# Attention with a learned distance bias and two feed-forward stages on one core: two query buffers, late clearing of probability tiles, smaller rings in the bias stretch

## The chip, the cores and the metric

The kernel runs on one core of one Trainium2 chip. The metric is the device time of one execution in microseconds (us). The core has TensorE (PE; PEld is its weight load), VectorE (DVE), ScalarE (ACT), GpSimd (POOL) and SyncE (SP), each with its own instruction queue worked off in order, and 16 DMA engines that share what is issued. In this kernel SyncE issues every transfer.

## What is computed

Attention over 2 batches, 8 heads, 576 positions, head size 64, with a bias that a small network makes from the distance of two positions, and then two feed-forward stages on the 1152 rows of 512. All is float32.

```python
scores = scale * np.matmul(q, k.transpose(0, 1, 3, 2))
psi_rel = np.log1p(np.abs(rel))                       # rel = i - j
psi_i = np.log1p(np.maximum(pos[:, None], 1.0))
x = (psi_rel / psi_i)[..., None]
h = np.maximum(x @ w1 + b1, 0.0)                      # 32 hidden units
bias = h @ w2                                         # one value per head
scores = scores + bias.transpose(2, 0, 1)[None, :, :, :]
attn = softmax(scores)
x = attn @ v                                          # rows of 8 heads x 64 = 512
x = (silu(x @ w_gate) * (x @ w_val)) @ w_out          # 512 -> 1536 -> 512
out = softplus(x @ w_in) @ w_out2                     # 512 -> 2048 -> 512
```

## The kernel before

**Precision.** Matmuls run on pairs of reduced-precision tiles: a high part and a remainder (`kst` holds both halves of the keys, `qh` and `ql` the queries' two parts). `high` is a cast on ScalarE or VectorE, `low` a subtraction, mostly on GpSimd.

**The bias stretch.** 36 blocks, in the order 32 to 35 and then 0 to 31. For each block `hidden` writes four tiles `r` (three on VectorE, the fourth on ScalarE) from a table `G`; `second` multiplies them with the second layer's weights, eight matmuls into a PSUM tile `pb` of two; `keep` scales `pb` on ScalarE into a tile `st` and has SyncE send it off. `r` comes from a pool `rp` of 12 buffers, `st` from `stp` of 4; a buffer is written again when its last reader is done, for `st` when its transfer has landed. `hidden` runs two blocks ahead, and its `r` on ScalarE stands ahead of the `st` of the block two back. The first four blocks go to a tensor `last` in device memory and come back, other way round, by two `bias<-last` transfers that wait for all four; the other 32 go straight to the tiles `bias` (0 to 3), eight to each.

**Attention.** Eight units, each one pair of heads of one batch. A unit has keys `kr` (two transfers of 288 KB), queries `qr` (two of 288 KB), values `v` (256 KB) and `vt` (32 KB). It has two halves (`sub` 0 and 1) of four and five slots. A slot does the scores of one 128-row chunk into `ps`, adds the bias and takes the row minimum on VectorE (`biased`, writes a tile `e` of 128x640 of which 576 columns are used), exponentials on ScalarE, and the normalization on GpSimd (`softmax`). Later slots transpose `e` (`transposes`, `gather`) and multiply by the values (`values`). The transposes read the 64 columns behind the 576th too, so these hold zeros. There are 14 tiles `e`, five of them from the start, nine after the bias stretch, in the room of `G`, `r` and `st`; each tile's last columns are cleared on GpSimd when the tile is made (line 128).

**What runs where.** The first five slots of unit 0 are run inside the bias stretch, behind the blocks numbered 23, 26, 31, 33 and 35 (`EARLY`). `prep` is a generator with the casts and subtractions of the next half's `kst`, `qh` and `ql`; two of its steps go into each slot. The order on TensorE, ScalarE, VectorE and GpSimd is that of the program text; SyncE's order is a scheduler's.

**Loads.** `kr` and `qr` have one buffer each (pool `qkraw`). `load_k` of the next unit is called at the first slot of a unit, `load_qv` (queries and values) at the first slot of its second half.

After attention come the weight stages: 68 weight tiles are loaded, turned into two parts and multiplied on TensorE. The change does not touch them.

Of the kernel before, what the change touches and what calls it, by code (L numbers as in the profile page):

```python
# [11 lines left out]
F32 = mybir.dt.float32  # L12
# [7 lines left out]
P = 128  # L20
B, H, S, D, HID = 2, 8, 576, 64, 32
# [64 lines left out]
def tile_kernel(ctx: ExitStack, tc, qT, kT, vS, wb, wg, wv, wo, wi, wo2, table, out):  # L86
    nc = tc.nc
# [13 lines left out]
    def opener(stack):  # L101
        return lambda name, bufs, **k: stack.enter_context(
            tc.tile_pool(name=name, bufs=bufs, reuse_waits="tile", **k)
        )

    with ExitStack() as actx:
        pool = opener(actx)
        biasp = pool("biasp", 1)
        bias = [biasp.tile([P, H, S], F32, name=f"bias{c}") for c in range(4)]
        bias.append(biasp.tile([P, NP, S], F32, name="bias4"))  # L110
        rawp = pool("qkraw", 1)
        kp = pool("kp", 2)
        qp = pool("qp", 1)
        vp = pool("vp", 2)
# [6 lines left out]
        es = []  # L121

        def new_es(name, count):

            ep = pool(name, 1)
            for _ in range(count):
                es.append(ep.tile([P, 5 * P], F32, name=f"e{len(es)}"))
                nc.gpsimd.memset(es[-1][:, S:], 0.0)

        new_es("ep0", 5)  # L130
        psS = pool("psS", 2, space=PSUM)

        def load(r, src, pr, b):
            for d in range(2):
                sp.dma_start(
                    out=r[D * d : D * (d + 1)], in_=src[b, 2 * pr : 2 * pr + 2].rearrange("h d s -> d h s")
                )

        def load_k(pr, b):
            kr = rawp.tile([P, 2, S], F32, tag="kr", name="kr")  # L140
            load(kr, kT, pr, b)
            return dict(pr=pr, b=b, kr=kr)

        def load_qv(u):
            pr, b = u["pr"], u["b"]
            u["qr"] = rawp.tile([P, 2, S], F32, tag="qr", name="qr")
            load(u["qr"], qT, pr, b)
            v = u["v"] = vp.tile([P, 4, P], F32, name="v")
            vt = u["vt"] = vts[(pr * B + b) % 3]
            sp.dma_start(out=v, in_=vS[b, pr, :512].rearrange("(c p) e -> p c e", p=P))  # L150
            sp.dma_start(out=vt[:64], in_=vS[b, pr, 512:])

        def high(h, src, by="a"):
            if by == "a":
                nc.scalar.copy(h, src)
            else:
                nc.vector.tensor_copy(h, src)

        def low(l, h, src, by="p"):
            eng = nc.gpsimd if by == "p" else nc.vector  # L160
            eng.tensor_tensor(l, src, h.bitcast(F32), op=ALU.subtract)

        def prepare_k(u):


            kst = u["kst"] = kp.tile([P, 2, S], F32R, tag="kst", name="kst")
            kr = u["kr"]
            for a in range(2):
                high(kst[:, a], kr[:, a], KHIGH[a])
                yield  # L170
                for hf in range(2):
                    rows, cols = slice(D - D * hf, P - D * hf), slice(HALF * hf, HALF * (hf + 1))
                    low(kst[rows, a, cols], kst[rows, a, cols], kr[rows, a, cols], KLOW[2 * a + hf])
                yield

        def prepare_q(u, sub):


            qr = u["qr"]
            width = 704 if sub else 512  # L180
            qh = qp.tile([P, width], F32R, tag=f"qh{sub}", name="qh")
            ql = qp.tile([P, width], F32R, tag=f"ql{sub}", name="ql")
            sm = smp.tile([P, 4, 5], F32, name="sm")
            if sub == 0:
                parts = [(0, 0, 0, 256), (1, 256, 0, 256)]
                chunks = [(0, 0), (0, 1), (1, 0), (1, 1)]
            else:
                parts = [(0, 0, 256, 320), (1, 448, 256, 256), (1, 384, 512, 64)]
                nc.gpsimd.memset(qh[:, 320:384].bitcast(F32), 0.0)
                nc.gpsimd.memset(ql[:, 320:384].bitcast(F32), 0.0)  # L190
                chunks = [(0, 0), ("mix",), (1, 0), (0, 1), (1, 1)]
            u[sub] = dict(u, sub=sub, qh=qh, ql=ql, chunks=chunks, sm=sm, es=[])
            for j, (a, o, s0, w) in enumerate(parts):
                high(qh[:, o : o + w], qr[:, a, s0 : s0 + w], QHIGH[2 * sub + j])
                yield
                low(ql[:, o : o + w], qh[:, o : o + w], qr[:, a, s0 : s0 + w], QLOW[2 * sub + j])
                yield

        sctx = actx.enter_context(ExitStack())
        pool = opener(sctx)  # L200
        gp = pool("gp", 1)
        rp = pool("rp", 12)
        stp = pool("stp", 4)
        psB = pool("psB", 2, space=PSUM)
        dramp = sctx.enter_context(tc.tile_pool(name="dramp", bufs=1, space=bass.MemoryType.DRAM))
        last = dramp.tile([64, H, S], F32, name="last")
# [79 lines left out]
        def biased(u, n, ps, bt):  # L286

            made[0] += 1
            e = es[made[0] % 14]
            nc.vector.tensor_tensor_reduce(  # L290
                out=e[:, :S].rearrange("p (a n) -> p a n", a=2),
                in0=ps[:, :, :HALF],
                in1=bt.rearrange("p (a n) -> p a n", a=2),
                op0=ALU.add,
                op1=ALU.min,
                scale=-0.125,
                scalar=3.0e38,
                accum_out=u["sm"][:, 0, n : n + 1],
            )
            u["es"].append(e)  # L300
# [8 lines left out]
        made = [-1]  # L309
# [12 lines left out]
        def gather(u, jc, pts):  # L322
            at = atp.tile([P, 640], F32, name="at")
            o = 0
            for pt, w in pts:
                if w < 512 or (u["sub"] == 0 and jc == 3):
                    nc.vector.tensor_copy(at[:, o : o + w], pt[:, :w])  # L327
                else:
                    nc.scalar.copy(at[:, o : o + w], pt[:, :w])  # L329
                o += w  # L330
            return at
# [17 lines left out]
        def finish(u):  # L349
            pr, b, sub, po = u["pr"], u["b"], u["sub"], u["po"]  # L350
            n = 320 if sub else 256
            xh, xl = xT
            cols = slice(S * b + 256 * sub, S * b + 256 * sub + n)
            nc.vector.tensor_copy(xh[:, pr, cols], po[:, :n])
            nc.vector.tensor_tensor(xl[:, pr, cols], po[:, :n], xh[:, pr, cols].bitcast(F32), op=ALU.subtract)  # L355
# [1 line left out]


        units = [load_k(0, 0)]
        load_qv(units[0])  # L360
        chunks = [(i, sub, n) for i in range(2 * NP) for sub in range(2) for n in range(4 + sub)]
        jobs, turned, gathered, done = [], [], [], []
        prep = itertools.chain(prepare_k(units[0]), prepare_q(units[0], 0))
# [3 lines left out]
        def run_slot():  # L367
            nonlocal turned, done, prep, before, slot
            if slot < len(chunks):
                i, sub, n = chunks[slot]  # L370
                if n == 0:
                    for _ in prep:
                        pass
                    if sub == 0:
                        if i + 1 < 2 * NP:
                            units.append(load_k((i + 1) // B, (i + 1) % B))
                        prep = prepare_q(units[i], 1)
                    elif i + 1 < 2 * NP:
                        load_qv(units[i + 1])
                        prep = itertools.chain(prepare_k(units[i + 1]), prepare_q(units[i + 1], 0))  # L380
                u = units[i][sub]
                got = scores(u, n)
            for w in done:
                finish(w)
            done = []
            for t in turned:
                t.append(gather(*t))
            if slot < len(chunks):
                biased(u, n, *got)
            if before:  # L390
                softmax(*before)
                before = None
            for _ in range(2):
                next(prep, None)
            held, turned = turned, []
            for _ in range(2 if slot % 9 == 8 or slot >= len(chunks) else 1):
                if jobs and jobs[0][2] <= slot:
                    w, jc, _ = jobs.pop(0)
                    turned.append([w, jc, transposes(w, jc)])
            gathered.extend(held)  # L400
            ends = [i + 1 for i, (_, jc, _, _) in enumerate(gathered) if jc in TOGETHER]
            for _ in range(max(ends, default=0)):
                w, jc, _, at = gathered.pop(0)
                values(w, jc, at)
                if jc == 4:
                    done.append(w)
            if slot < len(chunks):
                before = (u, n)
                if n == 3 + sub:
                    jobs.extend((u, jc, slot + LAG) for jc in range(5))  # L410
            slot += 1

        order = [32, 33, 34, 35, *range(32)]
        with tc.manual_schedule(engines={E.PE, E.Activation, E.DVE, E.Pool}):
# [19 lines left out]
            pool = opener(actx)  # L434
# [10 lines left out]
    units = []  # L445
# [12 lines left out]
    rawp = mpool("rawp", 3)  # L458
# [164 lines left out]
```

## Time and profile before

| | |
|---|---|
| time, median of 3 runs | 645.27 us (643.32 to 645.98) |
| the profiled execution's time | 645.52 us |
| its span, first to last instruction | 643.7 us |
| mean granted TensorE clock | 0.992 |
| busy: TensorE, VectorE, ScalarE, GpSimd | 617.8, 387.8, 318.9, 194.7 us |
| bias stretch: ScalarE's first and last `st` | 8.38 and 69.04 us |
| scores of attention's unit 1 begin | 77.84 us |

The page gives busy time for each engine over the whole span, and a chain of work that ended last. For a change that acts in one stretch, the views by window, the chain in order of time, and the timeline of one engine say more than the totals. In a timeline row, what stands in brackets is the engine's idle time before the row and what ended it. A row of SyncE (SPq) is the issue of a transfer, not the transfer.

### The profile page before, as it was taken

To read this page: it belongs to the slowest core of one execution; us is meant where nothing else is said; L and a number is where in the kernel's file an instruction comes from. 1 tells how busy PE (TensorE), PEld (TensorE's weight loads), DVE (VectorE), ACT (ScalarE), POOL (GpSimd) and SP (SyncE) were. 2 spreads that over 40 slices of the span, in tenths; PEclk is the share of its full clock that TensorE was granted. 3 is DMA by queue.
4 is the path that set the end of the run, shared out by engine and by line. 5 is a ranking of instruction groups with operands and counts; after the bars stand their busy time and mean duration, and the time that the engine had idled before them with its cause. 6 is when DMAs were issued, how large, how long until landed. Compare 5 with 4: busy or idle time off the path is not lost.

```text
span 643.7 us, 11124 instructions
## 1 busy us (share of the span) xinstructions
PE 617.8 (96%) x4128; PEld 559.6 (87%) x4128; DVE 387.8 (60%) x887; ACT 318.9 (50%) x623; POOL 194.7 (30%) x243
## 2 busy tenths in 40 slices
PE   8688799999998899999999999999999999999997
PEld 5233577777876799999999999999999999999997
DVE  7899778988886896575665734344654444542111
ACT  6588767777776553434434332225664213664000
POOL 1202677777772432221312221212122121221000
PEclk9899999999999999999999999999999999999999
DMA  8989722333421544224232232222323223200111
GB/s 245 192 202 209 176 74 66 84 93 94 92 82 36 165 161 141 89 69 127 67 109 90 70 127 71 94 92 73 98 66 99 69 95 98 67 1 0 38 60 51
DMA packets 53317, 63.29 MB, mean 98 GB/s; under 512 B 2832, under 2 KB 43792, under 8 KB 53264
## 3 DMA queue, kind: packets, MB, share of 16 engines
q1 hardware_dynamic: 53264, 62.59, 35.0%
q8 instruction: 32, 0.52, 0.4%
q14 instruction: 21, 0.17, 0.1%
HBM read 49.60 MB, written 3.54 MB: 83 GB/s over the span
## 4 chain that ended last, share of the span: by engine, by line
PE 81%; ACT 8%; DMA 5%; DVE 3%; issue 2%; SPq 0%; POOL 0%; ACTq 0%; DVEq 0%; POOLq 0%
PE pm L512 66%; PE po L341 6%; PE pt L318 4%; DMA bias<-st 3%; PE ps L277 3%; ACT e L304 3%; PE pb L238 2%; ACT at L329 2%; ACT st L250 2%; PE warm L417 1%; DMA qr<-in_qT_dram 1%; ACT r L228 1%; DVE at L327 1%; DMA last<-st 1%; DVE x L485 0%
## 5 line engine op out<-in xcount | busy, mean ns | idle before, releaser
L491 POOL TENSOR_TENSOR wl<-x,wh 128x512 fp32r<-128x512 f32 x68 | 88.9, 1313 | 293.2 <-ACT wh L490 172.1
L512 PE MATMUL pm<-xh,wh 128*128 128x384 f32 x480 | 160.5, 334 | 1.3 <-DVE xl L355 1.3
L512 PE MATMUL pm<-xh,wl 128*128 128x384 f32 x480 | 160.3, 334 | 0.0
L512 PE MATMUL pm<-xl,wh 128*128 128x384 f32 x480 | 160.3, 334 | 0.0
L483 ACT ACTIVATE u<-raw 128x512 f32<-128x512 f32 x68 | 45.8, 675 | 120.1 <-DVE x L486 77.5
L485 DVE TENSOR_SCALAR x<-u 128x512 int32<-128x512 int32 x68 | 40.0, 588 | 99.4 <-POOL wl L491 98.1
L512 PEld LDWEIGHTS pm<-xh,wh 128*128 128x128 f32 x480 | 90.1, 188 | 1.7 <-issue 1.6
L512 PEld LDWEIGHTS pm<-xl,wh 128*128 128x128 f32 x480 | 90.1, 188 | 0.0
L512 PEld LDWEIGHTS pm<-xh,wl 128*128 128x128 f32 x480 | 90.1, 188 | 0.0
L490 ACT CAST wh<-x 128x512 fp32r<-128x512 f32 x68 | 42.1, 620 | 62.1 <-PE pm L512 50.0
L307 POOL TENSOR_SCALAR e<-e,sm 128x576 f32<-128x576 f32 x72 | 55.0, 764 | 52.8 <-DVE sm L306 46.2
L512 PE MATMUL pm<-g2h,wl 128*128 128x384 f32 x192 | 64.1, 334 | 0.0
L512 PE MATMUL pm<-g2h,wh 128*128 128x384 f32 x192 | 64.1, 334 | 0.0
L512 PE MATMUL pm<-g2l,wh 128*128 128x384 f32 x192 | 64.1, 334 | 0.0
L318 PE MATMUL pt<-ident,e 128*128 128x128 f32 x360 | 56.2, 282 | 7.6 <-ACT at L329 4.0
L304 ACT ACTIVATE e<-e,sm 128x576 f32<-128x576 f32 x72 | 56.1, 779 | 8.1 <-DVE sm L290 5.7
L238 PE MATMUL pb<-r,wb_sb 128*32 128x288 f32 x576 | 49.9, 435 | 9.3 <-ACT st L250 7.3
L290 DVE CUSTOM_DVE_ANT_0 e<-ps,bias 128x576 f32<-128x576 f32 x72 | 54.0, 750 | 5.0 <-PE ps L277 4.7
L329 ACT COPY at<-pt 128x512 f32<-128x512 f32 x72 | 41.1, 581 | 31.0 <-PE pt L318 30.8
L318 PEld LDWEIGHTS pt<-ident,e 128*128 128x128 f32 x360 | 41.2, 141 | 17.5 <-ACT at L329 8.1
L488 DVE SCALAR_TENSOR_TENSOR x<-raw,x 128x512 int32<-128x512 int32 x68 | 53.3, 783 | 1.6
L230 DVE TENSOR_SCALAR r<-G 128x576 f32<-128x576 f32 x108 | 51.8, 551 | 3.6 <-PE pb L238 3.5
(64 smaller groups left out, 1036.7 us busy)
## 6 DMA issues: line engine op xcount, KB each, us to landing
raw<-in_wo_dram SPq DMA_DIRECT2D x28, 512.0 KB, 3.4
bias<-st SPq DMA_DIRECT2D x32, 288.0 KB, 4.6
raw<-in_wi_dram SPq DMA_DIRECT2D x16, 512.0 KB, 3.5
raw<-in_wg_dram SPq DMA_DIRECT2D x12, 512.0 KB, 3.6
raw<-in_wv_dram SPq DMA_DIRECT2D x12, 512.0 KB, 3.6
kr<-in_kT_dram SPq DMA_DIRECT2D x16, 288.0 KB, 4.4
qr<-in_qT_dram SPq DMA_DIRECT2D x16, 288.0 KB, 4.2
out_dram<-acc SPq DMA_DIRECT2D x12, 192.0 KB, 1.9
```

Source lines behind the costliest of these rows:

```text
L230: nc.vector.tensor_scalar(r, G[:, w0 : w0 + S], PB[:, n : n + 1], 0.0, op0=ALU.add, op1=ALU.max)
L238: nc.tensor.matmul(pb[32 * ct : 32 * ct + 32, hf, :HALF], W2, rs[ct][:, HALF * hf : HALF * (hf + 1)], start=True, stop=True,)
L290: nc.vector.tensor_tensor_reduce(out=e[:, :S].rearrange("p (a n) -> p a n", a=2), in0=ps[:, :, :HALF], in1=bt.rearrange("p (a n) -> p a n" ...
L304: nc.scalar.activation(e, e, AF.Exp, bias=sm[:, 0, n : n + 1], scale=-1.0, accum_out=sm[:, 1, n : n + 1])
L307: nc.gpsimd.tensor_scalar(e, e, sm[:, 3, n : n + 1], 1.0, op0=ALU.mult, op1=ALU.mult)
L318: nc.tensor.transpose(pt[:, P * w : P * (w + 1)], u["es"][i][:, P * jc : P * (jc + 1)], ident)
L329: nc.scalar.copy(at[:, o : o + w], pt[:, :w])
L483: nc.scalar.activation(u, hw.bitcast(F32), AF.Copy, scale=2.0**-112)
L488: nc.vector.scalar_tensor_tensor(x, lw, 29, x, op0=ALU.logical_shift_right, op1=ALU.bitwise_or)
L490: nc.scalar.copy(wh, x.bitcast(F32))
L491: nc.gpsimd.tensor_tensor(wl, x.bitcast(F32), wh.bitcast(F32), op=ALU.subtract)
L512: nc.tensor.matmul(ps[:, :n], w[:, k], x, start=first and k == 0 and i == 0, stop=last and k == NK - 1 and i == 2)
```

## The change

Queries get a pool of their own, `qrp`, with two buffers; `load_q` of the next unit is called together with `load_k`, and `load_v` stays where `load_qv` was. The 4,608 bytes that this takes of each partition come from the bias stretch: `rp` has 11 buffers instead of 12 and `stp` 3 instead of 4. The clearing of a tile `e` is moved from the place where the tile is made to the slot that first uses it.

```diff
         rawp = pool("qkraw", 1)
+        qrp = pool("qraw", 2)
@@
                 es.append(ep.tile([P, 5 * P], F32, name=f"e{len(es)}"))
-                nc.gpsimd.memset(es[-1][:, S:], 0.0)
@@
-        def load_qv(u):
+        def load_q(u):
+            u["qr"] = qrp.tile([P, 2, S], F32, name="qr")
+            load(u["qr"], qT, u["pr"], u["b"])
+
+        def load_v(u):
             pr, b = u["pr"], u["b"]
-            u["qr"] = rawp.tile([P, 2, S], F32, tag="qr", name="qr")
-            load(u["qr"], qT, pr, b)
@@
-        rp = pool("rp", 12)
-        stp = pool("stp", 4)
+        rp = pool("rp", 11)
+        stp = pool("stp", 3)
@@
             e = es[made[0] % 14]
+            if made[0] < 14:
+                nc.gpsimd.memset(e[:, S:], 0.0)
@@
         units = [load_k(0, 0)]
-        load_qv(units[0])
+        load_q(units[0])
+        load_v(units[0])
@@
                             units.append(load_k((i + 1) // B, (i + 1) % B))
+                            load_q(units[i + 1])
                         prep = prepare_q(units[i], 1)
                     elif i + 1 < 2 * NP:
-                        load_qv(units[i + 1])
+                        load_v(units[i + 1])
```

On SyncE, from unit 0's queries to the first blocks of the bias stretch, the order before (`last` is the tensor in device memory, `bias_72` the first bias tile, `bias_76` the one that `last` fills):

```order
L135 DMA qr<-in_qT_dram 64x2x576 x2
L150 DMA v<-in_vS_dram 128x4x128
L151 DMA vt_92<-in_vS_dram 64x128
L150 DMA v<-in_vS_dram 128x4x128
L151 DMA vt_93<-in_vS_dram 64x128
L151 DMA vt_94<-in_vS_dram 64x128
L256 DMA last<-st 16x8x576 x4
L254 DMA bias_72<-st 16x8x576
L259 DMA bias_76<-last 64x4x576 x2
L254 DMA bias_72<-st 16x8x576 x7
```

The same place in the changed kernel:

```order
L135 DMA qr<-in_qT_dram 64x2x576 x2
L152 DMA v<-in_vS_dram 128x4x128
L153 DMA vt_95<-in_vS_dram 64x128
L135 DMA qr<-in_qT_dram 64x2x576 x2
L258 DMA last<-st 16x8x576 x3
L152 DMA v<-in_vS_dram 128x4x128
L258 DMA last<-st 16x8x576
L153 DMA vt_96<-in_vS_dram 64x128
L256 DMA bias_72<-st 16x8x576
L261 DMA bias_76<-last 64x4x576 x2
L256 DMA bias_72<-st 16x8x576 x7
```

Unit 1's queries stand ahead of the four `last<-st`, its `v` between the third and the fourth, one `vt` behind the fourth; the third `vt` goes behind the bias stretch.

On GpSimd, where the bias stretch ends and unit 1's first `ql` is made, the order before (`e_112` is the tile of slot 4, `e_978` that of slot 5; six more memsets like the three shown first stand in the row where lines are left out):

```order
L161 TENSOR_TENSOR kst<-kr,kst 64x288 x2
L128 MEMSET e_978 128x64
L128 MEMSET e_980 128x64
L128 MEMSET e_982 128x64
...
L307 TENSOR_SCALAR e_112<-e_112,sm 128x576
L161 TENSOR_TENSOR kst<-kr,kst 64x288
L307 TENSOR_SCALAR e_978<-e_978,sm 128x576
L161 TENSOR_TENSOR ql<-qr,qh 128x256
```

The same place in the changed kernel (`e_111` and `e_981` are those two tiles):

```order
L163 TENSOR_TENSOR kst<-kr,kst 64x288 x2
L293 MEMSET e_981 128x64
L311 TENSOR_SCALAR e_111<-e_111,sm 128x576
L163 TENSOR_TENSOR kst<-kr,kst 64x288
L293 MEMSET e_982 128x64
L311 TENSOR_SCALAR e_981<-e_981,sm 128x576
L163 TENSOR_TENSOR ql<-qr,qh 128x256
```

Of nine memsets in a row one stays there, one stands before the next normalization, and seven come behind this `ql`.

## Rows read from the trace of the kernel before

**Rows 1.** The page: the chain that ended last, shares by engine.
```profile
PE 81%; ACT 8%; DMA 5%; DVE 3%; issue 2%; SPq 0%; POOL 0%; ACTq 0%; DVEq 0%; POOLq 0%
```

**Rows 2.** Busy us and instructions by stretch; last: granted clock, DMA share, GB/s.
```profile
8.00:10.00 2.00, 1.96 (x23) 0.79 (x18) 2.00 (x5) 1.62 (x3) 0.00 (x0) 1.00 1.05 243
18.00:20.00 2.00, 1.93 (x20) 0.62 (x16) 2.00 (x4) 2.00 (x4) 1.51 (x2) 1.00 0.48 61
30.00:32.00 2.00, 2.00 (x24) 0.84 (x20) 1.27 (x3) 1.75 (x3) 0.00 (x0) 0.50 1.07 211
78.00:80.00 2.00, 1.49 (x9) 1.25 (x9) 1.97 (x7) 1.87 (x5) 1.84 (x3) 0.69 0.93 252
80.00:82.00 2.00, 2.00 (x10) 1.42 (x10) 1.57 (x8) 1.64 (x4) 1.53 (x5) 0.50 0.06 12
300.00:643.00 343.00, 340.31 (x1964) 339.99 (x1962) 149.79 (x258) 122.78 (x236) 60.82 (x47) 1.00 0.24 75
```

**Rows 3.** Chain of waits, 8 to 36 us: start, length, what.
```profile
13.52 4.07 DMA last<-st
...
17.68 0.54 SPq L259
...
18.98 8.70 DMA bias<-st
...
27.77 0.75 ACT st L250
```

**Rows 4.** The first `last<-st`: its issue on SyncE, and us to landing.
```profile
9.14 0.57 SPq L256 DMA_DIRECT2D last<-st  x1
...
last<-st SPq DMA_DIRECT2D x1, 288.0 KB, 5.0
```

**Rows 5.** Timeline of ScalarE: some of the 36 `st`; start, length.
```profile
19.50 0.73 ACT L250 ACTIVATE st<-pb,G 128x576 f32<-128x576 f32 x1
...
27.77 0.74 ACT L250 ACTIVATE st<-pb,G 128x576 f32<-128x576 f32 x1 [6.31 <-DMA bias<-st]
...
36.00 0.73 ACT L250 ACTIVATE st<-pb,G 128x576 f32<-128x576 f32 x1
...
43.74 0.75 ACT L250 ACTIVATE st<-pb,G 128x576 f32<-128x576 f32 x1
...
49.92 0.73 ACT L250 ACTIVATE st<-pb,G 128x576 f32<-128x576 f32 x1
...
58.86 0.74 ACT L250 ACTIVATE st<-pb,G 128x576 f32<-128x576 f32 x1 [2.06 <-DMA bias<-st]
...
69.04 0.75 ACT L250 ACTIVATE st<-pb,G 128x576 f32<-128x576 f32 x1 [0.54 <-PE pb L238]
```

**Rows 6.** Transfers `bias<-st` issued between 33.6 and 40 us.
```profile
DMA to landing us min/median/max: 3.7/3.9/4.3
```

**Rows 7.** Transfers `bias<-st` issued between 59.7 and 70 us.
```profile
DMA to landing us min/median/max: 3.8/4.1/4.4
```

**Rows 8.** Timeline of the handover to unit 1, rows of three engines.
```profile
73.72 0.83 POOL L128 MEMSET e<- 128x64 f32 x9
...
76.59 0.31 DVE L157 CAST qh<-qr 128x256 fp32r<-128x256 f32 x1 [2.40 <-DMA qr<-in_qT_dram]
...
76.99 0.73 POOL L161 TENSOR_TENSOR ql<-qr,qh 128x256 fp32r<-128x256 f32 x1 [0.23 <-DVE qh L157]
...
77.84 0.19 PEld L277 LDWEIGHTS ps<-kst,ql 128*128 128x128 f32 x1 [2.07 <-POOL ql L161]
```

**Rows 9.** Chain of waits: transposes and scores at the handover, and later.
```profile
79.16 1.12 PE pt L318 x4
80.27 0.96 PE ps L277 x4
...
107.86 0.66 PE pt L318 x4
108.85 0.52 PE ps L277 x4
```

## Prediction

> **What bounds the kernel now.** I read the page first, then busy time by stretch, then the chain of waits where a stretch is not full of TensorE work. The page's chain is 81% TensorE with DMA at 5% and ScalarE at 8% [rows 1]: over the whole span the matmuls set the end. By stretch it divides. From 300 us on TensorE is busy 340.31 of 343 us [rows 2], and the attention and weight stages before that are nearly as full; the diff leaves their matmuls alone. The change acts in the first 80 us: the bias stretch (36 blocks, up to about 69 us) and the handover to unit 1 of attention (69 to 82 us).
>
> In the bias stretch the chain is not TensorE but the ring of `st` tiles. ScalarE writes an `st`, SyncE sends it off (288 KB), and the buffer is free when the transfer has landed. The chain shows the fourth `last<-st`, 4.07 us to landing, then the two `bias<-last` issues behind it at 17.68, then one `bias<-st` that took 8.70 us to land, and only then ScalarE's next `st` at 27.77 [rows 3]. ScalarE had written the one before at 19.50 [rows 5]: it stood still for 6.31 us because the four buffers were all in a queue of DMA work. From 24 us on the DMA engines are busy throughout (the stretch 30 to 32 us has a share of 1.07 at 211 GB/s [rows 2]). A 288 KB block is 294,912 bytes, at 211 GB/s 1.40 us of that queue. In quieter times ScalarE is the limit, with a block every 1.29 us (36.00 to 43.74, six steps [rows 5]). The same wait comes back at 58.86, 2.06 us, behind the load of the second unit's keys.
>
> At the handover VectorE waits 2.40 us for `qr`, and TensorE's next scores wait 2.07 us for `ql` [rows 8].
>
> **Part by part, in us against the profiled execution's 645.5** (span 643.7 plus 1.8 around it; the median of the three runs, 645.27, is 0.25 lower, so I take 0.25 off at the end).
>
> *Loads moved forward.* In the order now, SyncE issues unit 1's two `qr` loads right after unit 0's loads, ahead of the four `last<-st`; one `v` load goes behind the third of these, a `vt` load behind the fourth and another to after the bias stretch. So 576 KB of queries stand ahead of the first `last<-st` where 256 + 32 + 32 KB stood: 256 KB more, at 243 GB/s (8 to 10 us [rows 2]) 1.08 us. The first `last<-st` was issued at 9.14 and landed 5.0 later, at 14.1 [rows 4]; now about 15.2.
>
> *`st` from four buffers to three.* Then the fourth `st`, written at 12.77 before (0.75 ahead of its transfer's issue at 13.52 [rows 3]), has no buffer of its own; it needs the first one's landing: 15.2 + 0.1 to start, 0.74 to write, so it is issued at 16.1 and, with the same 4.07 as before, lands at 20.1. Both `bias<-last` wait for it, and stand in SyncE's queue ahead of every later `bias<-st`: 20.2 instead of 17.68, **+2.5** (A). If the 256 KB cost nothing, the buffer wait alone gives 14.1 + 0.1 against 12.77, +1.4: that is the lower end. From there to the first landing the queue is full of DMA work and can only shift as a whole.
>
> At the end of that jam three buffers come out one block further back: the landing that let ScalarE write its tenth `st` at 27.77 now lets it write the ninth (done at 19.50 before). One block of the full queue is **+1.4** (C).
>
> After the jam a ring of three may not turn faster than one landing allows. From the start of an `st` to its issue 0.76 and from landing to the next `st` 0.08 (27.68 to 27.77 [rows 3]). Landings were 3.7, 3.9 and 4.3 (least, median, most) from 33.6 to 40 us and 3.8, 4.1 and 4.4 from 59.7 to 70 us [rows 6, 7]. With 3.9 the ring takes 4.74 for three blocks, 1.58 each; with four buffers it was 1.19, under ScalarE's own 1.29. What that costs, by stretches of ScalarE's rows [rows 5]: 36.00 to 43.74, six steps at 1.58 instead of 1.29, +1.7; 43.74 to 49.92, four steps, 6.3 instead of 6.2, +0.1; 58.86 to 69.04, seven steps, 11.1 instead of 10.2, +0.9. The other steps are already longer than 1.58 on average. Sum **+2.8** (B). With landings of 4.4 the pitch is 1.75 and the sum 2.8 + 0.8 + 2.1 = 5.7. Fewer transfers in flight can also land sooner; where they land within 3.0 the ring turns in 1.29 and B is 0. I take 3.9 because both stretches had a cadence near 1.5, the one that I expect now.
>
> The Trainium skill, "SBUF — State Buffer", section "The DMA setup-cost knee", gives a transfer as about 2 us plus its bytes at 436 GB/s. For 288 KB that is 2.7 us, an estimate from that page; by it the ring would turn in 1.2 us and B would be 0. The rows here, 3.7 at the least, speak against it.
>
> *The ring `r` from twelve to eleven.* The fourth `r` of block i+2, ScalarE's, now waits for the fifth matmul of block i. The `st` right behind it on ScalarE waits for all eight anyway, so this costs nothing while matmuls of a block take less than two blocks' time.
>
> *The handover.* `qr` is there long before, so the 2.40 us on VectorE go. What is late next is GpSimd: between the memsets at 73.72 and the end of its first `ql` of unit 1 (starting at 76.99, 0.73 long) it was idle only 0.23 us [rows 8]. Of the nine memsets that stood in that row (0.83 in all, 0.09 each) seven go behind that `ql`, 0.65. So the scores start 0.65 + 0.23 = 0.9 sooner. The half clock may go as well: after the gap the granted clock was 0.69 and 0.50 [rows 2], the 1.2 GHz level for most of it, and four transposes took 1.12 and the scores 0.96, where the same pieces take 0.66 and 0.52 later on [rows 9]: 0.9 in all. The gap shrinks by half, so I take half of this, 0.5. Handover **-1.4** (T). Ends: 0.8 (GpSimd alone, some of it lost) and 2.07 + 0.9 = 3.0 (the whole gap and the clock).
>
> *Memsets elsewhere.* Five go from the start, where nothing waits for them, into slots where GpSimd idles; seven cost 0.09 each among later GpSimd work that TensorE covers. Nothing. The later `qr` loads come earlier than a unit needs them; no row between 84 and 190 us gave a wait for `qr`, so there is nothing to gain there.
>
> Sum: 2.5 + 1.4 + 2.8 - 1.4 = +5.3, so 645.5 + 5.3 - 0.25 = **650.6**, rounded.
>
> **The rivals.**
> *The ring is free.* Fewer transfers in flight land within 3.0, B is 0: 2.5 + 1.4 - 1.4 = +2.5, **647.8**, within 0.5%. For it: landing times contain queueing. Against: 3.7 is the least in two calm stretches. Chance 0.19. The page's figure above would give this case.
> *Not slower: the queries fit into idle DMA time.* The share was 0.48 from 18 to 20 us [rows 2], while SyncE waited for `last`. If the extra bytes vanish there, `bias<-last` is not moved, the ring is free, and the whole gap and the half clock go at the handover: -3.0, **642.3**. It decides if `bias<-last` is issued before 18 us. Against: the fourth `st` cannot be written before the first has landed. Chance 0.08, most of it just over the bound of 0.5%.
> *The ring is worse.* Landings of 4.4: 2.5 + 1.4 + 5.7 - 0.8 = +8.8, **654.0**. For it: 4.4 occurs in the calm stretch [rows 7], and the extra loads make it less calm. Longer gaps may also cost clock: at 30 to 32 us, after the jam, 0.50 was granted [rows 2]. Chance 0.16.
>
> **How the numbers follow.** The forecast has 0.57, and of this a little lies under 648.5. Range: 646.0 leaves out the not-slower case, and 654.2 takes in the worse ring. About 0.5% (3.2 us) is what a measurement of this kernel can tell from no change: slower by more than that 0.73, within it 0.20, faster 0.07.
>
> **What would show it.** In the changed kernel: `bias<-last` issued near 20.2 (A); the ninth `st` written near 30.3 (C); steps of ScalarE's `st` near 1.58 with ScalarE waiting for `bias<-st`, where they were 1.29 (B), and the last `st` near 75.7 instead of 69.04; no wait for `qr`, the scores of unit 1 some 7.9 us behind the last `st` instead of 8.8 (T). Wrong would be steps of 1.29 in the middle of the stretch (B is 0), or `bias<-last` at 18 us. From then on both kernels should take the same time to the end.

## The result, and the profile after

The changed kernel takes 651.18 us (median of 6 runs, 650.58 to 652.58) against 645.16 us of the kernel before: 1.0105 times as long, 95% interval 1.0092 to 1.0117. That is +6.8 us by the ratio (5.9 to 7.5). The forecast was 650.6 us, +5.3, and slower by more than 0.5%: 650.6 is close to 651.2, but +5.3 lies below the measured interval.

The profiled execution of the changed kernel has a span of 648.8 us, 5.1 more than before, and took 650.58 us. The chain that ended last, on its page, by engine:

```profile
PE 79%; ACT 7%; DMA 5%; DVE 4%; issue 3%; POOL 1%; ACTq 0%; SPq 0%; POOLq 0%; DVEq 0%
```

Little moves there, as little is moved outside the first 90 us: the last 343 us are the same to 0.1 us of TensorE work (compare the last row of [rows 2]). Busy time by stretch, with the granted clock, DMA share and GB/s at the end of each row:

```profile
62.00:64.00 2.00, 0.00 (x0) 0.00 (x0) 2.00 (x5) 0.27 (x1) 1.15 (x3) 1.00 0.99 196
66.00:68.00 2.00, 2.00 (x20) 0.85 (x16) 1.22 (x4) 1.24 (x3) 0.00 (x0) 0.50 0.83 221
82.00:84.00 2.00, 1.75 (x12) 1.27 (x12) 2.00 (x3) 1.18 (x3) 2.00 (x4) 1.00 0.00 0
84.00:86.00 2.00, 1.19 (x9) 1.00 (x9) 1.93 (x10) 1.63 (x4) 2.00 (x5) 1.00 0.62 166
305.00:648.00 343.00, 340.36 (x1964) 340.03 (x1962) 151.16 (x261) 123.95 (x238) 61.01 (x47) 1.00 0.24 75
```

SyncE's timeline, answering to [rows 3]: the fourth `last<-st`, and the two `bias<-last` behind it. The fourth store landed 3.0 us after its issue.

```profile
16.54 0.52 SPq L258 DMA_DIRECT2D last<-st  x1
...
19.67 1.20 SPq L261 DMA_DIRECT2D bias<-last  x2
```

ScalarE's timeline, answering to [rows 5]: the fourth, ninth, tenth, fifteenth, 21st, 25th, 28th, 29th and last `st`. In brackets stands ScalarE's idle time before the row and what ended it.

```profile
15.78 0.74 ACT L252 ACTIVATE st<-pb,G 128x576 f32<-128x576 f32 x1 [2.94 <-DMA last<-st]
...
29.58 0.74 ACT L252 ACTIVATE st<-pb,G 128x576 f32<-128x576 f32 x1 [5.87 <-DMA bias<-st]
31.46 0.73 ACT L252 ACTIVATE st<-pb,G 128x576 f32<-128x576 f32 x1
...
39.92 0.72 ACT L252 ACTIVATE st<-pb,G 128x576 f32<-128x576 f32 x1
...
49.95 0.74 ACT L252 ACTIVATE st<-pb,G 128x576 f32<-128x576 f32 x1 [1.08 <-DMA bias<-st]
...
55.75 0.72 ACT L252 ACTIVATE st<-pb,G 128x576 f32<-128x576 f32 x1
...
63.73 0.74 ACT L252 ACTIVATE st<-pb,G 128x576 f32<-128x576 f32 x1 [2.26 <-DMA bias<-st]
65.05 0.74 ACT L252 ACTIVATE st<-pb,G 128x576 f32<-128x576 f32 x1
...
76.93 0.74 ACT L252 ACTIVATE st<-pb,G 128x576 f32<-128x576 f32 x1 [0.95 <-DMA bias<-st]
```

Before, the fourth `st` had no wait, as its row in the kernel before shows, and the last one came at 69.04.

```profile
12.77 0.73 ACT L250 ACTIVATE st<-pb,G 128x576 f32<-128x576 f32 x1
```

Now the fourth waits 2.94 us for the first store's landing, the queue's jam ends with the ninth `st`, not the tenth, and ScalarE waits for `bias<-st` again and again (seven times, 11.3 us in all up to 90 us, where it was twice and 8.4).

The transfers `bias<-st` land a little sooner than before [rows 6, 7]; issued between 37.3 and 55 us, and then between 64.6 and 78 us:

```profile
DMA to landing us min/median/max: 3.3/3.6/4.6
```

```profile
DMA to landing us min/median/max: 3.2/3.3/3.8
```

The handover, answering to [rows 8], rows of three engines:

```profile
81.99 1.48 DVE L159 CAST qh<-qr 128x256 fp32r<-128x256 f32 x1
...
84.04 0.72 POOL L163 TENSOR_TENSOR ql<-qr,qh 128x256 fp32r<-128x256 f32 x1
...
84.81 0.19 PEld L279 LDWEIGHTS ps<-kst,ql 128*128 128x128 f32 x1 [1.17 <-POOL ql L163]
```

VectorE no longer waits for `qr`. TensorE's first weight load of unit 1 waits 1.17 us instead of 2.07 for GpSimd's `ql`; it comes 7.88 us behind the last `st` instead of 8.80, and the clock stays at 1.00 behind it, where it had been 0.69 and 0.50. VectorE's cast of `qh` now takes 1.48 us, where it took 0.31 [rows 8]. It still ends before GpSimd comes to `ql` (84.04), so it is not what TensorE waits for.

A balance of the two traces: the last `st` comes 7.9 us later (76.93 against 69.04). From there to the first `po` matmul (the values of unit 0) it is 9.75 us instead of 12.12 (86.68 and 81.16), 2.4 less, and 0.5 more is won between that and the first matmul of the weight stages (132.49 us apart instead of 132.95). Together +5.1, the difference of the spans. That is less than the +6.8 that was measured: the traced execution of the changed kernel is the fastest of its six, and that of the kernel before, 645.52, is above its median.

### The profile page after: what moved, and what is told of

The parts are those of the page before. It is cut to its first block, busy times and chain, and to the rows that moved or that the text cites. A ratio compares the mean times of both kernels' runs of the same rounds, so it can differ in the third digit from the quotient of the medians.

```text
span 648.8 us, 11153 instructions
## 1 busy us (share of the span) xinstructions
PE 615.3 (95%) x4128; PEld 557.1 (86%) x4128; DVE 388.9 (60%) x887; ACT 319.9 (49%) x623; POOL 196.1 (30%) x243
## 4 chain that ended last, share of the span: by engine, by line
PE 79%; ACT 7%; DMA 5%; DVE 4%; issue 3%; POOL 1%; ACTq 0%; SPq 0%; POOLq 0%; DVEq 0%
PE pm L518 65%; PE po L345 6%; DMA bias<-st 4%; PE pt L322 4%; ACT e L308 3%; PE ps L279 3%; ACT at L333 2%; PE pb L240 2%; DVE r L232 1%; ACT st L252 1%; DVE at L331 1%; DMA G<-in_table_dram 1%; DVE x L491 0%; POOL kst L163 0%; ACT r L230 0%
## 5 line engine op out<-in xcount | busy, mean ns | idle before, releaser
L240 PEld LDWEIGHTS pb<-r,wb_sb 128*32 128x32 f32 x576 | 18.8, 118 | 46.9 <-ACT st L252 32.1
```

The lines of the kernel that those rows point to most:

```text
L240: nc.tensor.matmul(pb[32 * ct : 32 * ct + 32, hf, :HALF], W2, rs[ct][:, HALF * hf : HALF * (hf + 1)], start=True, stop=True,)
```

## The experiments

**My theory** was that the ring of three `st` makes the time, in three ways (start, jam, pitch), and that the queries' early load gives back a part at the handover. **The rivals:** the queries' 576 KB ahead of the stores make the time; the ring of `r` does; or GpSimd's row of memsets is what the handover waited for. Each ratio is to the kernel before, run on the same chip beside it.

| kernel | `stp` / `rp` / query buffers | median us | ratio (95%) |
|---|---|---|---|
| changed | 3 / 11 / 2 | 651.18 | 1.0105 (1.0092 to 1.0117) |
| e1_stp3 | 3 / 12 / 1 | 652.18 | 1.0126 (1.0106 to 1.0146) |
| e2_rp11 | 4 / 11 / 1 | 645.15 | 1.0013 (0.9998 to 1.0028) |
| e3_late_clear | 4 / 12 / 1 | 643.96 | 0.9999 (0.9987 to 1.0011) |
| e4_stp4_rp10 | 4 / 10 / 2 | 645.00 | 1.0012 (1.0001 to 1.0022) |
| e5_hole | 4 / 10 / 2 | 647.37 | 1.0043 (1.0027 to 1.0059) |
| e9_hole_act | 4 / 10 / 2 | 644.44 | 0.9992 (0.9979 to 1.0006) |
| e6_one_buffer_slot3 | 4 / 12 / 1 | 645.26 | 1.0010 (0.9996 to 1.0024) |
| e6_one_buffer_slot2 | 4 / 12 / 1 | 644.38 | 0.9991 (0.9977 to 1.0005) |
| e7_stp2 | 2 / 12 / 1 | 669.24 | 1.0381 (1.0354 to 1.0408) |
| e8_stp5_rp11 | 5 / 11 / 1 | 644.62 | 0.9996 (0.9983 to 1.0009) |
| e10_after_bulk_clear | 3 / 11 / 2 | 652.69 | 1.0121 (1.0097 to 1.0146) |

### One part at a time

**e1_stp3**

```diff
-        stp = pool("stp", 4)
+        stp = pool("stp", 3)
```

> The kernel before with `stp` of 3 buffers, nothing else. Theory 1 (the st ring is the cost): the fourth st waits for the first landing (+1.4), the ninth st comes out of the jam where the tenth did (+1.4), and the rest of the stretch runs at the ring's pitch of about 1.55 (+4.2, as the changed kernel's trace has it): +7.0, about 652, no gain at the handover since the queries still come late. Theory 2 (the cost is the 576 KB of queries that moved ahead of the stores): at most +2, about 647.

Measured +8.1 by the ratio (6.8 to 9.4). One buffer of `st` alone costs as much as the whole change, or a little more (its queries come as late as before, so it lacks the handover's gain). Its trace shows the same three places: the start, the jam, and waits in the calm part (ScalarE; fourth, ninth, tenth, 20th and 21st, and last `st`).

```profile
15.06 0.74 ACT L250 ACTIVATE st<-pb,G 128x576 f32<-128x576 f32 x1 [2.35 <-DMA last<-st]
...
29.27 0.74 ACT L250 ACTIVATE st<-pb,G 128x576 f32<-128x576 f32 x1 [6.92 <-DMA bias<-st]
31.15 0.73 ACT L250 ACTIVATE st<-pb,G 128x576 f32<-128x576 f32 x1
...
46.66 0.74 ACT L250 ACTIVATE st<-pb,G 128x576 f32<-128x576 f32 x1 [0.26 <-DMA bias<-st]
50.18 0.74 ACT L250 ACTIVATE st<-pb,G 128x576 f32<-128x576 f32 x1 [2.12 <-DMA bias<-st]
...
76.22 0.74 ACT L250 ACTIVATE st<-pb,G 128x576 f32<-128x576 f32 x1 [0.80 <-DMA bias<-st]
```

`bias<-last` was issued at 18.86 here, 17.68 before and 19.67 in the changed kernel: by these three traces 1.2 of the 2.0 us of this term are the buffer's and 0.8 those of the queries ahead of the stores. The split is rough: e10 below has the same order of transfers as the changed kernel, and its `bias<-last` was issued at 20.25.

**e2_rp11**

```diff
-        rp = pool("rp", 12)
+        rp = pool("rp", 11)
```

> The kernel before with `rp` of 11 buffers, nothing else. Theory 1: no effect, 645.2 within 0.7, because the r of ScalarE waits for the fifth matmul of a block whose eighth the st behind it needs anyway. Rival (the r ring is part of the cost, ScalarE waited 4.6 us for pb's matmuls in front of r in the changed kernel): +2 or more, 647 or more.

Measured no difference that is clear of zero (-0.1 to +1.8), and the rival's +2 lies outside. e1, with twelve `r`, costs no less than the changed kernel with eleven, which fits. The waits that ScalarE shows in the changed kernel in front of `r` (4.6 us in 9) are time it would have waited behind it.

**e3_late_clear**

```diff
-                nc.gpsimd.memset(es[-1][:, S:], 0.0)
...
             e = es[made[0] % 14]
+            if made[0] < 14:
+                nc.gpsimd.memset(e[:, S:], 0.0)
```

> The kernel before with the clearing of the e tiles at first use, nothing else. Theory 1: the queries land at 76.5 us whatever GpSimd does, so 0 to -0.3, 645.0. Rival (GpSimd's row of memsets is what the handover waits for): -0.65 or more, 644.5.

Measured no difference (-0.8 to +0.7). The interval does not part 0 from -0.65 cleanly, but the trace does: GpSimd stands idle for 0.44 us in front of the first `ql`, where it was 0.23 [rows 8], and waits for VectorE's cast, which starts at 75.61, as soon as the queries have landed (the second transfer was issued at 70.5 and took 5.0 us).

```profile
75.99 0.73 POOL L160 TENSOR_TENSOR ql<-qr,qh 128x256 fp32r<-128x256 f32 x1 [0.44 <-DVE qh L156]
```

With the queries late, GpSimd's row is not what ends last.

**e10_after_bulk_clear**, the changed kernel with that part undone:

```diff
+                nc.gpsimd.memset(es[-1][:, S:], 0.0)
...
             e = es[made[0] % 14]
-            if made[0] < 14:
-                nc.gpsimd.memset(e[:, S:], 0.0)
```

> The changed kernel with the e tiles cleared where they are made, as before; two query buffers, `rp` 11, `stp` 3. Theory 1 (with the queries there in time GpSimd's row is what the handover waits for): the first values matmul 10.3 to 10.5 behind the last st instead of 9.75, +0.6 against the changed kernel, 651.8. Rival (clearing never matters): 651.2, handover 9.75.

The nine memsets are back in a row on GpSimd, ahead of the first `ql`:

```profile
80.95 0.83 POOL L129 MEMSET e<- 128x64 f32 x9
81.77 0.77 POOL L310 TENSOR_SCALAR e<-e,sm 128x576 f32<-128x576 f32 x1
...
84.04 0.72 POOL L164 TENSOR_TENSOR ql<-qr,qh 128x256 fp32r<-128x256 f32 x1
...
86.51 1.95 PE L344 MATMUL po<-at,v 128*64 128x256 f32 x16
```

The first `po` matmul comes 10.23 us behind the last `st` (76.28) instead of 9.75: 0.5 of the 0.65 that the prediction gave. In the time it is lost in the spread: the two kernels' intervals overlap.

### How many buffers

**e7_stp2**

```diff
-        stp = pool("stp", 4)
+        stp = pool("stp", 2)
```

> The kernel before with `stp` of 2. If the ring sets the pitch, two blocks take 0.84 plus a landing of 3.3, a step of 2.07: from the tenth st to the last 26 steps are 54 instead of 41.3, and with the start and the jam two buffers further back the total is +15 to +18, 660 to 663. If a shorter ring only moves waits about in a queue that is full anyway, no more than twice what `stp` 3 cost without its jam terms: below 656.

Measured +24.6 (22.8 to 26.3, from two runs), three times e1 and more than I had worked out. Landings are down to 3.2 us in the median, and the calm part shows the ring turning once every 4.07 us for two blocks, 2.03 each, as 0.84 + 3.2 gives (ScalarE's `st` between 44 and 54 us):

```profile
44.02 0.74 ACT L250 ACTIVATE st<-pb,G 128x576 f32<-128x576 f32 x1 [1.33 <-DMA bias<-st]
45.48 0.74 ACT L250 ACTIVATE st<-pb,G 128x576 f32<-128x576 f32 x1
48.09 0.74 ACT L250 ACTIVATE st<-pb,G 128x576 f32<-128x576 f32 x1 [1.21 <-DMA bias<-st]
49.52 0.74 ACT L250 ACTIVATE st<-pb,G 128x576 f32<-128x576 f32 x1
52.13 0.74 ACT L250 ACTIVATE st<-pb,G 128x576 f32<-128x576 f32 x1 [1.21 <-DMA bias<-st]
```

Others were longer: the mean of all 26 steps from the tenth (34.33) to the last (93.65) is 2.28. I did not part what of that excess belongs to the keys' loads and what to the half clock that the trace shows in four stretches after the jam.

**e8_stp5_rp11**

```diff
-        rp = pool("rp", 12)
-        stp = pool("stp", 4)
+        rp = pool("rp", 11)
+        stp = pool("stp", 5)
```

> The kernel before with `stp` of 5 and `rp` of 11. Theory 1 (four buffers already keep the DMA queue full, so the queue sets the pace and only fewer buffers cost): within 0.7 of the kernel before, 645, with landings longer by about a block. Rival (every buffer counts, as from two to three to four): -2 or more.

Measured no difference (-1.1 to +0.6). Landings of `bias<-st` issued from 20 to 70 us, first in the kernel before, then with five buffers:

```profile
DMA to landing us min/median/max: 3.7/4.6/10.9
```

```profile
DMA to landing us min/median/max: 5.1/5.8/11.1
```

The fifth buffer adds 1.2 us to the median landing and takes nothing off the end. So the sequence of buffers is 2, 3, 4, 5: +24.6, +8.1, 0, 0. Below four the ring sets the pitch. From four on it does not: from the fifteenth `st` to the 21st a step is 1.29 us with four buffers and 1.33 with five, and ScalarE waits for no landing there.

### Where the handover's gain goes

**e4_stp4_rp10**, the changed kernel with other rings:

```diff
-        rp = pool("rp", 11)
-        stp = pool("stp", 3)
+        rp = pool("rp", 10)
+        stp = pool("stp", 4)
```

> The changed kernel with `stp` of 4 and `rp` of 10 (the room is the same). Theory 1: the extra 256 KB ahead of the stores cost about 1.1, the ring costs nothing, the handover gains 2.8: -1.7, about 643.5 (642.5 to 645), bias<-last issued near 18.8 us. Theory 2 (the loads are the cost): still slower than the kernel before, 648 or more. If an r ring of 10 holds VectorE back, ScalarE's st steps in the calm part grow from 1.29 to 1.5 or so and the time stays above 646.

Measured +0.8 (0.1 to 1.4): the loss is gone with the fourth `st`, and so is theory 2, but my -1.7 did not come either. The handover is as short as in the changed kernel (9.75 us again, 71.50 to 81.25); the bias stretch lost as much as that gains (its last `st` is 2.5 us later than before). `bias<-last` comes at 19.81 behind a `last<-st` that took 5.7 us to land:

```profile
13.25 0.58 SPq L152 DMA_DIRECT2D v<-in_vS_dram  x1
13.97 0.52 SPq L258 DMA_DIRECT2D last<-st  x1
16.56 0.56 SPq L256 DMA_DIRECT2D bias<-st  x1
19.81 1.23 SPq L261 DMA_DIRECT2D bias<-last  x2
```

I had counted the bytes ahead of the first `last<-st`. Unit 1's `v`, gone from there, stands ahead of the fourth one, and that is what `bias<-last` waits for: 2.1 us later than before, not 1.1. Of these 2.1, 0.45 are there when the fourth store is issued, and this trace's first `st` came 0.86 later than the one before (9.24 and 8.38); how much of that the loads make is not shown.

**e5_hole** and **e9_hole_act** put unit 1's queries behind the four `last<-st`, with e4's rings. A copy of two columns from the fourth `st` into the query tile makes the load wait; the load then overwrites them. In e5 GpSimd makes the copy, in e9 ScalarE.

```diff
+        def load_q_behind(st):
+            qr = qrp.tile([P, 2, S], F32, name="qr")
+            nc.gpsimd.tensor_copy(qr[:, :, :1], st[:, :2].rearrange("p (a n) -> p a n", a=2))
+            load(qr, qT, 0, 1)
+            early.append(qr)
```

> As e4 (two query buffers, `stp` 4, `rp` 10), but unit 1's queries are made to wait for the fourth st, so that they stand behind the four last<-st and ahead of bias<-last, where the DMA engines had a share of 0.48. Theory 1 (e4 lost its gain to the queries ahead of the stores): bias<-last back near 17.9 (e4 19.8), handover as in e4, about 1.5 faster than e4, 643. Rival (the queue is work that shifts as a whole wherever the 576 KB stand): as e4, 645.

e5 did not test what it was made for. The copy took 4.46 us on GpSimd, the queries were issued at 18.26 and stood in front of `bias<-last` after all (19.77); +2.8 (1.7 to 3.8).

```profile
13.77 4.46 POOL L155 COPY qr<-st 128x2 f32<-128x2 f32 x1 [11.80 <-ACT st L263]
```

> e5 again with the small copy that ties the queries to the fourth st on ScalarE; in e5 it ran on GpSimd, took 4.46 us there, and the queries were issued at 18.26 instead of 14. Theory 1 (there is idle DMA time between the last store and bias<-last): queries issued near 14.3, bias<-last near 17.9, the jam ends within 1 of the kernel before's, the handover is 2.4 shorter: 643 or a little less, 2 faster than e4. Rival (the queue shifts as a whole wherever the 576 KB stand): the tenth st at 29.5 or later, 645 to 646.

e9 did. The queries go out at 14.32 and `bias<-last` at 17.60, as early as before:

```profile
9.59 4.64 SPq L269 DMA_DIRECT2D last<-st  x4
14.32 1.96 SPq L135 DMA_DIRECT2D qr<-in_qT_dram  x2
17.60 1.20 SPq L273 DMA_DIRECT2D bias<-last  x2
18.84 10.48 SPq L267 DMA_DIRECT2D bias<-st  x5
```

Yet the time is that of the kernel before, -0.5 (-1.4 to +0.4): the tenth `st` comes at 29.91, not 27.77, and the last at 71.03, 2.0 later, and against the trace of the kernel before the handover gives 2.4 back. The idle DMA time did fill, from a share of 0.48 [rows 2] to 0.96:

```profile
18.00:20.00 2.00, 1.66 (x24) 0.66 (x20) 2.00 (x4) 2.00 (x4) 1.59 (x2) 1.00 0.96 192
```

But in the kernel before the first `bias<-st` was issued at 15.00, ahead of `bias<-last`, and now stands behind it. So the rival's numbers held: 576 KB more in this stretch cost about 2 us in both places that were tried, ahead of the stores (e4) and behind them (e9). In e9 the added bytes and the later `bias<-st` come together, and no run parts the two.

**e6_one_buffer_slot3** and **e6_one_buffer_slot2** leave the rings of the kernel before and the one query buffer, and load the next unit's queries at the fourth or third slot of a unit, when the buffer is free, instead of the fifth. `e` is cleared at first use, as in e3. The loop over `prep` in the edit also runs the rest of the unit's casts and subtractions at once, as the buffer is free only behind them.

```diff
+                elif sub == 0 and n == 3 and i + 1 < 2 * NP:
+                    for _ in prep:
+                        pass
+                    load_q(units[i + 1])
```

> One query buffer and the rings of the kernel before (`rp` 12, `stp` 4); e cleared at first use; the next unit's queries are loaded at the fourth slot of a unit, when the buffer is free, instead of the fifth: two blocks before the end of the bias stretch. Theory 1 (room for a second buffer was never needed, the handover gain is to be had without it): the queries land some 4 us sooner, the handover is 2 shorter, the last two st land up to 1.5 later: -1.5, 643. Rival (queries among the last stores hold up the bias that slots 7 and 8 need): 645 or more.

> The same with the load at the third slot, four blocks before the end. Theory 1: like e6_one_buffer_slot3 or up to 0.5 better, as the four last blocks have more time behind the queries: 642.5 to 643.5. Rival: the ring waits once more for the 2.8 us of queries, as it does for the keys: 645 to 647.

Neither differs from the kernel before (-0.3 to +1.5 and -1.5 to +0.3). The handover is as long as in the trace of the kernel before (12.08 and 11.81 us to the first `po`). VectorE's timeline of the first of the two shows why: the wait for `qr` shrinks from 2.40 to 0.77, and a wait for the last bias rows, whose transfers stand behind the queries now, takes its place.

```profile
75.25 0.63 DVE L158 CAST qh<-qr 128x256 fp32r<-128x256 f32 x1 [0.77 <-DMA qr<-in_qT_dram]
77.53 0.76 DVE L293 CUSTOM_DVE_ANT_0 e<-ps,bias 128x576 f32<-128x576 f32 x1 [1.65 <-DMA bias<-st]
```

No version beat the kernel before by more than the measurement's spread.

## Why the prediction was right, point by point

- **Sign and mechanism** held: one `st` buffer less is the loss (e1), the ring of `r` is nothing (e2), the clearing is next to nothing (e3, e10). The not-slower rival needed `bias<-last` before 18 us and fell with its 19.67, and again with e9; the rival of a free ring fell with e1 and e7.
- **The sum held in part by luck.** In the two traces the bias stretch was forecast at +6.7 and came to +7.9; the handover was forecast at -1.4 and gave -2.8. These two errors offset each other, and +5.3 meets the +5.1 of the spans. Over all runs the change cost +6.8 (5.9 to 7.5), more than forecast: the loss was undersized, and T below shows that the larger gain belongs to this one trace of the kernel before.
- **A** (forecast +2.5, measured +2.0, `bias<-last` at 19.67). The step that I took over from the trace as a constant, 4.07 us for the fourth store to land, was 3.0. Against that the first store landed at 15.7, 0.5 later than forecast, 6.7 us behind its issue. The part for the loads was worked out from the bytes ahead of the first store; with four buffers the fourth store counts, as e4 showed.
- **A and C together** were forecast at 3.9 for the tenth `st`; it came 3.7 later (31.46 against 27.77), and the ninth at 29.58, forecast 30.3.
- **B** was undersized: +2.8 forecast, +4.2 measured from the tenth `st` to the last. The calm part was right: from the fifteenth `st` to the 25th the steps took 15.83 us instead of 13.92, +1.9 where +1.8 was forecast. (Fifteenth to 21st alone is 10.03 instead of 7.74, but the last of these six steps waits for a landing of 4.6 us, and the kernel before has a step of 2.17 just behind its 21st.) From the 25th to the 29th it was +0.4, from the tenth to the fifteenth +0.2, where nothing was forecast. Most of the error is in the last seven steps, +1.7 instead of +0.9. TensorE had been idle for all of 62 to 64 us, and the granted clock was 0.50 from 66 to 68, the 1.2 GHz level. The prediction named this as a danger and did not price it. e10's trace prices it: its bias stretch is that of the changed kernel but for the memsets, its clock stayed at 1.00 here, and its last seven steps (65.38 to 76.28) took 10.90 us, +0.7 against the kernel before, where the changed kernel took 11.88. So in this place the pitch is 0.7 and the half clock 1.0, by one trace of each. The rows of e10 are a stretch with its clock, and the first `st` of these steps:

```profile
66.00:68.00 2.00, 1.70 (x27) 0.70 (x28) 2.00 (x6) 2.00 (x4) 0.00 (x0) 1.00 0.82 205
```

```profile
65.38 0.74 ACT L253 ACTIVATE st<-pb,G 128x576 f32<-128x576 f32 x1
```

- **The landing as a constant.** I took 3.9 from a stretch with four transfers in flight. With three it was 3.3 to 3.6, with two 3.2 (e7). With five it was 5.8 over 20 to 70 us, where four gave 4.6 (e8); all are medians. By the page of the Trainium skill that the prediction cited, "SBUF — State Buffer", "The DMA setup-cost knee", 288 KB would be 2.7 us. The traces move toward that figure and stay 0.5 above it, and it would have given the wrong verdict. The 436 GB/s in that estimate is the Trainium skill's figure there for all 16 ports, and these transfers write 16 partitions of a tile.
- **T** was forecast at -1.4 and came to -2.8 against the trace of the kernel before. The scores start was right (0.92 sooner, 0.9 forecast). What came on top is that the clock stayed at 1.00, of which I had taken half, and that VectorE, freed of its wait, ran `biased` of two slots earlier, so that transposes and values followed the scores 1.87 us later instead of 3.32. I had followed GpSimd's row only. But half of the -2.8 is the half clock of that one trace. In e2 the queries come as late as in the kernel before, yet its clock stays at 1.00 from 74 to 82 us: the four transposes take 0.66 us, not 1.12, the sixteen `po` matmuls 1.95, not 2.43, and the first `po` comes 11.12 us behind the last `st`, not 12.12. Its last `st`, its transposes and its first `po`:

```profile
67.86 0.74 ACT L250 ACTIVATE st<-pb,G 128x576 f32<-128x576 f32 x1 [0.54 <-PE pb L238]
...
77.87 0.66 PE L318 MATMUL pt<-ident,e 128*128 128x128 f32 x4 [0.49 <-ACT at L329]
...
78.98 1.95 PE L341 MATMUL po<-at,v 128*64 128x256 f32 x16
```

Beside e2 the handover gives 1.4, the forecast's figure, and the changed kernel's last `st` is 9.1 us later, not 7.9. e3, also at full clock, has 10.84; e1, e8 and e6_one_buffer_slot3 fall to half clock here as the kernel before does. So T lies between -1.4 and -2.8 with the clock of the execution that it is set against.
- **What the prediction did not say** is that T's gain is paid for with queue time in the stretch before. It had the loads' price inside A, at 1.1 us; e4 and e9 put it at about 2, as much as the handover gives.

How much of B outside the last seven steps is the half clock that the ring's gaps bring stays open: no run held the clock. One more such place is 18 to 20 us, where the changed kernel has 0.55 after TensorE stood idle from 14 to 16, and the kernel before has 1.00 [rows 2].

## What to carry to other kernels

Before a buffer is taken from a ring that ends in a transfer, divide the ring's turn (write, issue, landing, back) by its buffers and set that beside the pitch of the engine that fills it: here 4.7 us over four was under 1.29 us and over three was not. Take the landing at the number of transfers that will be in flight, add the places where the ring has to ride out a jam, and expect the gaps to cost clock as well. Set a trace beside more than one execution of the kernel before: here one stretch at half clock in a single trace doubled what a part seemed to be worth. In this bias stretch, where the DMA engines were busy throughout from 20 to 34 us, an earlier load only changed which landing was late.

## What the runs showed of the hardware that I had not expected

A copy of two columns on GpSimd took 4.46 us while VectorE wrote its `r` tiles without a break (e5), where the same copy on ScalarE took 0.20 us (e9) and nine memsets of 64 columns on GpSimd 0.83 us together. VectorE was busy for the whole of it, 4.46 of 4.46 us from 13.77 to 18.23, with twelve operations and no gap:

```profile
13.77:18.23 4.46, 4.31 (x58) 1.90 (x60) 4.46 (x12) 4.44 (x7) 4.46 (x1) 1.00 0.50 162
```

The columns behind the length are PE, PEld, DVE, ACT and POOL busy, with the operations of each, and then the granted clock, the DMA share and GB/s. The other way round, VectorE's cast of `qh` in the changed kernel took 1.48 us, not 0.31, while GpSimd was busy for all of 82 to 84 us. The Trainium skill, "SBUF — State Buffer", section "Who interferes with whom", has VectorE and GpSimd share one pair of ports, which one of them holds as a lock while its instruction runs. Both rows fit that, but no run here separates it from another cause.
